# Squared-ReLU attention into a gated feed-forward block on one core: the third batch's transposing DMAs in a chain, its later loads one by one over the second batch, and two score buffers through the third batch

## The chip, the core and the metric

The kernel runs on one core of a Trainium2 chip. The metric is the time of one execution on the device in microseconds (us), median of several runs. Of the kernel before there are five runs, and one more execution that was profiled.

## The reference, cut to what matters

```python
# q, k, v: (8 batches, 12 heads, 448 rows, 64) float32
scores = (1 / sqrt(64)) * q @ k.T
attn = maximum(scores, 0) ** 2 / 448
x = (attn @ v), heads side by side: (8 * 448, 768)
# w_gate, w_val: (768, 1536); w_out: (1536, 768)
out = (gelu(x @ w_gate) * (x @ w_val)) @ w_out      # (3584, 768) float32
```

There is no softmax: a score needs nothing but its own square after the ReLU. The kernel works in bf16 with sums in float32.

## The kernel before, in words

**Stages and tiles.** The code counts batches b from 0 to 7, so the third batch is b = 2; heads are taken in pairs (pr 0 to 5), and two pairs make a group m (0 to 2). A batch passes through these steps:

- GpSimd issues the loads that cast to bf16: `load_qk` (L205; one DMA for q or for k and four heads, all in tile `qk16`) and `load_v` (L220; two DMAs for four heads of v).
- q and k are transposed. In batches 0 and 1 (`b < EARLY`, and `EARLY` is 2) TensorE does it (`add_transposes`, L362). From batch 2 on `add_dma_transposes` (L251) does it: VectorE copies a group from `qk16` into `qkr` (L261; one buffer for all batches), and then SyncE issues two transposing DMAs from `qkr` into `qkT` (L265), one of four and one of three chunks of 64 rows. The units of the group's scores wait for both.
- `add_scores` makes 21 units of scores for a batch (`NU`; units 0 to 6 belong to group 0, 7 to 13 to group 1, 14 to 20 to group 2). Each goes into a score buffer of two PSUM banks; ScalarE applies the ReLU (L425), VectorE squares (L431).
- `add_values` (L459) multiplies by v, a pair at a time; VectorE writes the result into `xT` (L487).
- `add_gate_value` (L519) makes gate and value for each of 12 slices `fc` of the hidden width. ScalarE applies the GELU (L538) and VectorE multiplies (L543); that multiply is `u_op[b, fc]`.
- `add_out` (L572) makes output tiles t of 128 rows in two halves g. ScalarE copies each half from PSUM (L598, `cp`), and after the second half SyncE issues two stores (L603). `osb` has four buffers.

**Two rows of work on TensorE.** Matmuls use 64 x 64 tiles of the array. The lower and upper halves of the rows get separate streams, `PE0` and `PE1`, which follow one another through a PSUM bank: the first half of a sum is made by the lower rows, the second by the upper rows (`then`, L351). While the upper rows finish one bank, the lower rows begin another.

**What sets the order.** All is planned in Python before anything is emitted. Every step of work has a place `at` in planned time (L657 to L705), in which only the feed-forward matmuls count: `starts[b]` is where batch b's feed-forward work begins, and the units of a batch's scores are spread evenly between `lo` and `hi` of L677 to L685. So attention for batch b + 1 lies among the feed-forward work for batch b. `run_plan` (L23) then plays the plan through with a cost for each operation and assumed arrival times of the DMAs. The streams `PE0` and `POOL` (GpSimd's loads) keep their listed order; from the lists of `PE1`, ScalarE, VectorE and SyncE it takes whichever operation is ready first. The order in which it takes them is the order of each engine's program, and every engine keeps to it. A DMA's assumed lateness is the `lag` of an operation, and the operation `wait` on the pretended engine `IDLE` (L254) puts a further 2 or 5 us ahead of a `qkr` copy in the plan. It exists in the plan alone.

**PSUM.** Eight banks: score buffer 0 (two banks), four banks F for all other results in a ring, and score buffer 1 (two banks). When the list `wide` is filled (L446), the kernel goes over to one score buffer, and the two banks of the other join as X, so that results go round six banks (`next_bank`, L302; `next_scores`, L316). Before the change that happens at the last unit of batch 1.

**Loads around the change.** The q and k of batch 2's groups 0 and 1 are issued at the end of the start-up loads (L652). Those of group 2 are issued after the copies of output tile 0, and v of batch 2 after tile 1 and after the multiplies of `fc` 1 and 3 of batch 1 (L613 to L616, L562). Each waits for that copy or multiply. Loads for batch 3 are issued after the even `fc` of batch 1 (q and k in turn, L557), and its v after `fc` 7, 9 and 11 (L564). The transposes of batch 2 are entered just ahead of its first scores (L709).

Of the kernel before, what the change touches and what calls it, by code (L numbers as in the profile page):

```python
# [88 lines left out]
def kernel(  # L89
# [16 lines left out]
    B, H, S, D = q.shape  # L106
# [4 lines left out]
    NM = NPAIR // 2  # L111
    NU = SC * NPAIR // 2
# [12 lines left out]
    EARLY = 2  # L125
# [33 lines left out]
    SYNC = mybir.DependencyInfo(mybir.DependencyClass.Sync, mybir.DependencyReason.DATA)  # L159
# [17 lines left out]
    w12_op, wo_op, head_op = {}, {}, {}  # L177
# [61 lines left out]
    qkT, tr_op = {}, {}  # L239
# [7 lines left out]
        return t.rearrange("d (m c r) x -> d m c r x", m=NM, c=SC)  # L247

    qkr = {}

    def add_dma_transposes(b, m):  # L251


        wait = Op("IDLE", 2.0 if b == EARLY else 5.0, lambda: None,  # L254
                  [head_op[b, pr, i] for pr in (2 * m, 2 * m + 1) for i in range(2)])
        IDLE.append(wait)

        def emit_copy():
            if b not in qkr:
                qkr[b] = lpool.tile([128, NM, SC, 4, D], bf16, name="qkr", tag="qkr")  # L260
            nc.vector.tensor_copy(  # L261
                qkr[b][:, m], qk16[b].rearrange("p (h c d) -> p c h d", c=SC, d=D)[:, :, 4 * m:4 * m + 4])

        def emit_transpose(c0, c1):
            ins = nc.sync.dma_start_transpose(  # L265
                by_group(qkT_tile(b))[:, m, c0:c1].rearrange("d c r x -> d (c r) x"),
                qkr[b][:, m, c0:c1].rearrange("p c h d -> p (c h d)"))
            if b > EARLY:

                if c0:  # L270
                    tc.add_manual_dep(ins.ins, one[0].ins.name, SYNC, reason="pace")
                one[:] = [ins]

        one = []
        copy = Op("DVE", 0.65, emit_copy, [wait, *tr_op.get((b - 1, m), ())], lag=0.15, prio=3)
        DVE.append(copy)
        tr_op[b, m] = [Op("SP", 0.19 * 2 * (c1 - c0), lambda c0=c0, c1=c1: emit_transpose(c0, c1),
                          [copy, last_s.get(b - 2)], lag=4.5) for c0, c1 in ((0, VC), (VC, SC))]
        if b > EARLY:
            tr_op[b, m][1].deps.append(tr_op[b, m][0])  # L280
        SP.extend(tr_op[b, m])


# [114 lines left out]
    def add_scores(at, b, u):  # L398


        m, w = divmod(u, SC)
        tail = w == VC - 1
        prs = (2 * m, 2 * m + 1) if tail else (2 * m + (w > VC - 1),)
        cl = w if w < VC else w - VC
        box = {}
        n, free = next_scores()

        def emit(j, pr):
            if not box:
                box[0] = psS[n].tile([128, 2, 512], f32, name="sp", tag="S")  # L410
            sp = box[0]
            t = by_group(qkT_tile(b))[HALF[j], m, :, pr % 2, :]
            for i in range(2):
                if tail:
                    n0 = (pr % 2) * S // 2
                    qs = t[:, :, i * P // 2:(i + 1) * P // 2]
                    mm(sp[HALF[i], j, n0:n0 + S // 2].rearrange("k (c p) -> k c p", c=SC),
                       t[:, VC - 1, HALF[1]], qs, j, i, True, True)
                else:
                    mm(sp[HALF[i], j, 0:S].rearrange("k (c p) -> k c p", c=SC),  # L420
                       t[:, cl + i * VC, HALF[1]], t[:, :, HALF[0]], j, i, True, True)

        def emit_relu():
            rl = box[1] = rpool.tile([128, 2, S], bf16, name="rl", tag="rl")
            nc.scalar.activation(rl[:, :, :], box[0][:, :, 0:S], AF.Relu)  # L425

        def emit_sq():
            a = apool.tile([128, 2, S], bf16, name="attnT", tag="attnT")
            for pr in prs:
                att[b, pr, VC - 1 if tail else cl] = a  # L430
            nc.vector.tensor_tensor(a[:, :, :], box[1][:, :, :], box[1][:, :, :], op=ALU.mult)  # L431

        if b < EARLY:
            have = [t_op[b, m, pr % 2] for pr in prs]
        else:
            have = tr_op[b, m]
        have = [*have, *free]
        ops = [[Op(f"PE{j}", 0.095 if tail else 0.189, lambda j=j, pr=pr: emit(j, pr), have, lag=0.24)
                for pr in prs] for j in range(2)]
        last_s[b] = ops[1][-1]  # L440
        relu = Op("ACT", 0.8, emit_relu, [ops[0][-1], ops[1][-1], *sq_list[-4:-3]], lag=0.18, prio=2)
        n_a = len(sq_list)
        sq = Op("DVE", 0.54, emit_sq, [relu, *att_free[n_a - 12:n_a - 11]] if n_a >= 12 else [relu],
                lag=0.2, prio=2)
        scores_read(n, relu)
        if (b, u) == (EARLY - 1, NU - 1):  # L446
            wide.append(0)
        sq_list.append(sq)
        att_free.append(None)
        for pr in prs:  # L450
            sq_op.setdefault((b, pr), []).append((sq, n_a))
            sq_of[b, pr, VC - 1 if tail else cl] = sq
        ACT.append(relu)
        DVE.append(sq)
        both(at, zip(*ops))
# [60 lines left out]
    GS, RS = 0.189, 0.1625  # L516
    PLACE5 = -7.0

    def add_gate_value(at, b, fc, g):  # L519

        i, o = divmod(fc * 128, WCH)
        w = (wg, wv)[g][i]
        box = {}
        half, free = next_bank()

        def emit(r, dc):
            if not box:
                box[0] = new_bank(done, half=half)
            if r == 1 and dc == 0:
                wait_lower(box)  # L530
            for j in range(2):
                ins = mm(box[0][HALF[j], 0:S], w[HALF[r], dc, o + P * j:o + P * (j + 1)],
                         xT[b][HALF[r], dc, :], r, j, r == 0 and dc == 0, r == 1 and dc == KC - 1)
            box[1] = ins

        def emit_gelu():
            gel[b, fc] = gpool.tile([128, S], bf16, name="gel", tag="gel")
            nc.scalar.activation(gel[b, fc][:, :], box[0][:, 0:S], AF.Gelu)  # L538

        def emit_mult():  # L540
            if fc == 0:
                uT[b] = upool.tile([128, FC, S], bf16, name="uT", tag="uT")
            u_op[b, fc].ins = nc.vector.tensor_tensor(  # L543
                uT[b][:, fc, :], gel.pop((b, fc))[:, :], box[0][:, 0:S], op=ALU.mult).ins

        ops = [[Op(f"PE{r}", GS, lambda r=r, dc=dc: emit(r, dc),
                   [w12_op[i][g], x_op[b, dc], *(free if r == 0 and dc == 0 else ())], lag=0.24)
                for dc in range(KC)] for r in range(2)]
        if g == 0:
            done = gel_op[b, fc] = Op("ACT", 0.55, emit_gelu, [ops[1][-1]], lag=0.06, prio=0)  # L550
            ACT.append(done)
        else:
            done = u_op[b, fc] = Op("DVE", 0.54, emit_mult, [gel_op[b, fc], ops[1][-1]],
                                    lag=0.2, prio=0)
            DVE.append(done)
            if b + 2 < B and b:
                if fc % 2 == 0:  # L557
                    m, i = divmod(fc // 2, 2)
                    load_qk(b + 2, i, 4 * m, 4 * m + 4, [done])
                    if i:  # L560
                        add_dma_transposes(b + 2, m)
                elif b == 1 and fc < 5:  # L562
                    load_v(2, 2 * fc + 2, 2 * fc + 6, [done])
                elif fc > 6:  # L564
                    h0 = 2 * (fc - 7)
                    load_v(b + 2, h0, h0 + 4, [done])
        bank_read(half, done)
        if (b, fc) == (0, 0):
            at = [PLACE5 - 0.5 + 0.1 * g] * 3 + [0.01 * g] * 3
        then(at, GS, *ops, done)  # L570

    def add_out(at, t, g):  # L572
# [37 lines left out]
        cp = Op("DVE" if last else "ACT", 0.48, emit_copy, [ops[1][-1]], prio=1)  # L610
        bank_read(half, cp)
        (DVE if last else ACT).append(cp)
        if t == 0:  # L613
            load_qk(2, g, H - 4, H, [cp])
        elif (t, g) == (1, 0):
            load_v(2, 0, 4, [cp])  # L616
        if last and g != 1:

            part = slice(bounds[g and g - 1], bounds[g + 1])
# [40 lines left out]
    starts = []  # L660
# [14 lines left out]
    LEAD = 6.0  # L675
    LO1 = 2.0
    for b in range(B):  # L677
        if b == 0:
            lo, hi = -60.0, -12.0
        elif b == 1:  # L680
            lo, hi = LO1, starts[1] - LEAD
        elif b == 2:
            lo, hi = starts[1] + 6.0, starts[2] - LEAD
        else:
            lo, hi = starts[b - 1] - LEAD, starts[b] - LEAD  # L685
        step = (hi - lo) / NU
# [19 lines left out]


    for at, _, fn, args in work:
        if fn is add_scores and args == (2, 0):  # L709
            for m in range(NM):  # L710
                add_dma_transposes(2, m)
        fn(at, *args)


# [15 lines left out]
    for kind, lo, hi in pairs:  # L730
        if kind == "with":
            upper.append((tau[place[lo]], hi))
        else:
# [5 lines left out]
            t = tau[behind + 1]  # L739
# [48 lines left out]
```

## Time and profile before

| | us |
|---|---|
| median of five runs | 427.3 (425.7 to 428.2) |
| the profiled execution, its own time | 425.15 |
| its span, first to last instruction | 423.4 |

| in the profiled execution | start, us |
|---|---|
| multiplies of batch 1, fc = 0, 1, 2, 4, 7, 11 (L543) | 79.2, 81.7, 84.4, 89.5, 98.1, 109.6 |
| ReLU of batch 2's score units 0, 7, 14, 20 (L425) | 81.9, 94.4, 107.3, 118.1 |
| ReLU of batch 3's units 0, 7, 14 | 120.8, 136.7, 152.4 |
| copies into qkr for batch 2 (L261) | 67.9, 72.6, 78.2 |
| copies into qkr for batch 3 | 93.5, 104.9, 116.3 |
| transposing DMAs of batch 2 (L265) | 69.1, 73.4, 75.5, 77.4, 81.2, 83.5 |

The granted clock of TensorE is 0.998 of full speed over the span. In what follows a line of a wait gives the total wait in us, how often, and the longest; a line of a timeline or a chain gives start and length in us. A group's length runs from the start of its first instruction to the end of its last, so neighbouring groups overlap, since a matmul of 349 ns shares the array with others. A line of stretches gives the stretch, its length, and then for each engine busy us and, in brackets, the instructions.

### The profile page before, as it was taken

Reading aid. Unit: us, or ns where it says so; the run is one execution under the profiler, and the core shown is the slowest. Engines: PE = TensorE matmul, PEld = TensorE weight load, DVE = VectorE, ACT = ScalarE, POOL = GpSimd, SP = SyncE. Lnnn points to the kernel's source line nnn. Section 1 sums busy time; section 2 is a strip of 40 time slices with the busy share of each in tenths; the row PEclk is TensorE's granted clock in tenths of the full one; section 3 lists DMA queues with packets and bytes.
Section 4 is the critical chain, followed back from the end, with each engine's and each line's share of the span. In section 5 each row is a group of like instructions: output and inputs, shape, how many; then the busy total and the mean of one; then the engine's idle time right before and its main releaser. Section 6 shows DMA issues by size and latency. Waiting matters only on the chain.

```text
span 423.4 us, 19612 instructions
## 1 busy us (share of the span) xinstructions
PE 415.7 (98%) x9087; PEld 378.6 (89%) x9090; DVE 213.9 (51%) x347; ACT 223.7 (53%) x320; POOL 73.6 (17%) x120
## 2 busy tenths in 40 slices
PE   8999999999999999999999999999999999999996
PEld 3558778799999999999999989999999989999995
DVE  3876665266544665446643666446743555212201
ACT  4956663466556655556555665556555556322220
POOL 8645401223100131012300122011310000000000
PEclk9999999999999999999999999999999999999999
DMA  7999998999974399645974389645994100120034
GB/s 100 191 200 197 199 209 140 197 142 113 118 127 93 47 115 118 135 68 71 140 130 107 52 91 134 140 73 70 121 147 97 39 4 3 47 71 3 2 77 115
DMA packets 75281, 44.91 MB, mean 106 GB/s; under 512 B 36160, under 2 KB 71744, under 8 KB 75200
## 3 DMA queue, kind: packets, MB, share of 16 engines
q0 software_dynamic: 37152, 24.39, 43.2%
q1 hardware_dynamic: 37888, 19.08, 25.4%
q8 instruction: 71, 1.16, 1.2%
q10 hardware_dynamic: 160, 0.20, 0.1%
q14 instruction: 10, 0.08, 0.1%
HBM read 48.76 MB, written 11.01 MB: 141 GB/s over the span
## 4 chain that ended last, share of the span: by engine, by line
PE 93%; DMA 3%; POOL 1%; ACT 1%; issue 0%; DVE 0%; SPq 0%; POOLq 0%
PE ff L162 84%; PE sp L162 8%; DMA qkT<-qkr 2%; DMA qk<-in_k_dram 2%; PE sp L377 1%; POOL qk L214 1%; PE ff L377 1%; ACT rl L425 0%; PE ff L340 0%; SPq L603 0%; DVE qkT L381 0%; DVE attnT L431 0%; ACT osb L598 0%; DVE osb L598 0%; POOL ident masks.py:199 0%
## 5 line engine op out<-in xcount | busy, mean ns | idle before, releaser
L425 ACT ACTIVATE rl<-sp 128x896 bf16<-128x896 f32 x168 | 152.4, 918 | 93.0 <-PE sp L162 84.3
L162 PE MATMUL ff<-xT,wg 64*64 64x448 bf16 x2304 | 199.0, 349 | 0.0
L162 PE MATMUL ff<-xT,wv 64*64 64x448 bf16 x2304 | 197.9, 349 | 0.0
L162 PE MATMUL ff<-wo,uT 64*64 64x384 bf16 (+1 forms) x2736 | 151.5, 320 | 0.0
L431 DVE TENSOR_TENSOR attnT<-rl 128x896 bf16<-128x896 bf16 x168 | 104.0, 623 | 70.0 <-ACT rl L425 67.1
L162 PEld LDWEIGHTS <-wv 64*64 64x64 bf16 x2304 | 126.7, 107 | 6.9
L162 PEld LDWEIGHTS <-wg 64*64 64x64 bf16 x2304 | 125.5, 107 | 7.6
L162 PEld LDWEIGHTS <-uT 64*64 64x64 bf16 x2736 | 128.8, 107 | 3.1
L162 PE MATMUL sp<-qkT 64*64 64x448 bf16 (+1 forms) x768 | 105.3, 328 | 1.8 <-DMA qkT<-qkr 1.0
L543 DVE TENSOR_TENSOR uT<-gel,ff 128x448 bf16<-128x448 bf16 x96 | 59.5, 620 | 70.1 <-PE ff L162 63.2
L162 PE MATMUL ff<-attnT,v 64*64 64x448 bf16 (+1 forms) x768 | 88.5, 326 | 0.1
L538 ACT ACTIVATE gel<-ff 128x448 bf16<-128x448 f32 x96 | 52.0, 542 | 46.1 <-PE ff L162 45.6
L162 PEld LDWEIGHTS <-qkT 64*64 64x64 bf16 x768 | 46.2, 106 | 11.1 <-issue 5.6
L598 ACT COPY osb<-ff 128x384 f32<-128x384 f32 x54 | 25.7, 477 | 52.5 <-PE ff L162 52.5
L162 PEld LDWEIGHTS <-v 64*64 64x64 bf16 x768 | 47.8, 107 | 3.5 <-issue 1.1
L487 DVE TENSOR_SCALAR xT<-ff 128x448 bf16<-128x448 f32 x48 | 29.9, 623 | 34.0 <-PE ff L162 34.0
L214 POOL DMA_DIRECT2D qk<-in_q_dram x25 | 15.5, 621 | 125.9 <-DVE uT L543 105.6
L227 POOL DMA_DIRECT2D v<-in_v_dram x48 | 29.5, 621 | 42.7 <-DVE uT L543 33.2
L214 POOL DMA_DIRECT2D qk<-in_k_dram x25 | 15.4, 615 | 61.2 <-DVE uT L543 52.7
L261 DVE COPY qkr<-qk 128x1792 bf16<-128x1792 bf16 x18 | 19.4, 1078 | 4.5 <-DMA qk<-in_k_dram 4.5
L598 DVE COPY osb<-ff 128x192 f32<-128x192 f32 (+1 forms) x3 | 1.2, 422 | 17.9 <-PE ff L162 17.9
L377 PEld LDWEIGHTS <-qk 128*64 128x64 bf16 x168 | 5.2, 110 | 3.2 <-issue 3.1
(23 smaller groups left out, 41.7 us busy)
## 6 DMA issues: line engine op xcount, KB each, us to landing
out_dram<-osb SPq DMA_DIRECT2D x54, 192.0 KB, 2.8
v<-in_v_dram POOLq DMA_DIRECT2D x48, 128.0 KB, 4.9
qk<-in_q_dram POOLq DMA_DIRECT2D x23, 224.0 KB, 4.6
qk<-in_k_dram POOLq DMA_DIRECT2D x23, 224.0 KB, 5.3
wg<-in_moe_w_gate_dram POOLq DMA_DIRECT2D x6, 384.0 KB, 10.5
wv<-in_moe_w_val_dram POOLq DMA_DIRECT2D x6, 384.0 KB, 11.4
wo<-in_moe_w_out_dram POOLq DMA_DIRECT2D x4, 576.0 KB, 15.2
qkT<-qkr SPq DMA_TRANSPOSE x36, 4.7
```

The source lines that it names most:

```text
L162: return nc.tensor.matmul(o, lhsT, rhs, start=start, stop=stop, tile_position=(P * row, P * col))
L214: op = load(4 * (h1 - h0) * S * D, lambda: nc.gpsimd.dma_start(tile_of().rearrange("p (h x) -> p h x", h=H)[:, h0:h1, :], src[b, h0:h1].re ...
L227: return nc.gpsimd.dma_start(v16[b][HALF[i], h0:h1, :, :], v[b, h0:h1].rearrange("h (p c) d -> p h c d", c=SC)[:, :, c0:c0 + VC, :])
L261: nc.vector.tensor_copy(qkr[b][:, m], qk16[b].rearrange("p (h c d) -> p c h d", c=SC, d=D)[:, :, 4 * m:4 * m + 4])
L377: nc.tensor.transpose(t[HALF[j], c, :], src[:, 2 * (2 * m + r) + j, c, :], ident[:, :], tile_position=(0, P * j))
L425: nc.scalar.activation(rl[:, :, :], box[0][:, :, 0:S], AF.Relu)
L431: nc.vector.tensor_tensor(a[:, :, :], box[1][:, :, :], box[1][:, :, :], op=ALU.mult)
L487: nc.vector.tensor_scalar_mul(xT[b][:, pr, :], box[0][:, 0:S], scalar1=out_scale)
L538: nc.scalar.activation(gel[b, fc][:, :], box[0][:, 0:S], AF.Gelu)
L543: u_op[b, fc].ins = nc.vector.tensor_tensor(uT[b][:, fc, :], gel.pop((b, fc))[:, :], box[0][:, 0:S], op=ALU.mult).ins
L598: cp.ins = (nc.vector.tensor_copy if last else nc.scalar.copy)(osb[t][:, cols], box[0][:, 0:N]).ins
```

## The change

It has four parts.

1. *Transposes.* The list `one`, which holds the last transposing DMA, outlives a call. In batch 2 the DMAs of groups 1 and 2 each wait until the transposing DMA before them has landed, across groups too; group 0's two do not wait for one another. Later batches keep what they had: the second DMA of a group waits for the first. A call can be given operations (`deps`) that its planned wait comes after.
2. *Loads.* A table `LATE` names, for 17 places in the plan (copies of output tiles 0 to 5 and multiplies of batch 1), one load each, or one call of `add_dma_transposes`, or both. The last number of an entry says which: 0 for q, 1 for k, 2 for v, 3 for the transposes alone. So batch 2's third group of q and k comes after `fc` 0 and 1 of batch 1, its v after `fc` 2, 5 and 8, and batch 3's loads after `fc` 6, 7 and 9 and then after output tiles 2 to 5. Batch 2's transposes are entered at the copies of tiles 0 and 1 and at `fc` 4.
3. *Score buffers.* `wide` is filled at the last unit of batch 2 in place of batch 1: two score buffers and four F banks through batch 2.
4. *Place.* The units of batch 2's scores lie between `starts[1] + 8.0` and `starts[2] - 6.0`, where they began at `starts[1] + 6.0`.

```diff
-    def add_dma_transposes(b, m):
+    one = []
+    def add_dma_transposes(b, m, deps=()):
         wait = Op("IDLE", 2.0 if b == EARLY else 5.0, lambda: None,
-                  [head_op[b, pr, i] for pr in (2 * m, 2 * m + 1) for i in range(2)])
+                  [*deps] + [head_op[b, pr, i] for pr in (2 * m, 2 * m + 1) for i in range(2)])
...
-            if b > EARLY:
-
-                if c0:
-                    tc.add_manual_dep(ins.ins, one[0].ins.name, SYNC, reason="pace")
-                one[:] = [ins]
-
-        one = []
+            if b > EARLY and c0 or m and b == EARLY:
+                tc.add_manual_dep(ins.ins, one[0].ins.name, SYNC, reason="pace")
+            one[:] = [ins]
...
-        if b > EARLY:
+        if m or b > EARLY:
             tr_op[b, m][1].deps.append(tr_op[b, m][0])
+        if m and b == EARLY:
+            tr_op[b, m][0].deps.append(tr_op[b, m - 1][1])
...
-        if (b, u) == (EARLY - 1, NU - 1):
+        if (b, u) == (EARLY, NU - 1):
             wide.append(0)
...
+    LATE = {(0, 0): (2, 0, 3), (1, 0): (2, 1, 3), 0: (2, 2, 0), 1: (2, 2, 1), 2: (2, 0, 2),
+            4: (2, 2, 3), 5: (2, 1, 2), 6: (3, 0, 0), 7: (3, 0, 1), 8: (2, 2, 2), 9: (3, 1, 0),
+            (2, 0): (3, 1, 1), (3, 0): (3, 0, 2), (3, 1): (3, 2, 0), (4, 0): (3, 2, 1),
+            (5, 0): (3, 1, 2), (5, 1): (3, 2, 2)}
+
+    def load_late(b, m, i, done):
+        if i < 2:
+            load_qk(b, i, 4 * m, 4 * m + 4, done)
+        elif i == 2:
+            load_v(b, 4 * m, 4 * m + 4, done)
+        if i == 3 or i == 1 and b > EARLY:
+            add_dma_transposes(b, m, done if m else ())
...
-            if b + 2 < B and b:
+            if b == 1:
+                if fc in LATE:
+                    load_late(*LATE[fc], [done])
+            elif b + 2 < B and b:
                 if fc % 2 == 0:
                     m, i = divmod(fc // 2, 2)
                     load_qk(b + 2, i, 4 * m, 4 * m + 4, [done])
                     if i:
                         add_dma_transposes(b + 2, m)
-                elif b == 1 and fc < 5:
-                    load_v(2, 2 * fc + 2, 2 * fc + 6, [done])
...
-        if t == 0:
-            load_qk(2, g, H - 4, H, [cp])
-        elif (t, g) == (1, 0):
-            load_v(2, 0, 4, [cp])
+        if (t, g) in LATE:
+            load_late(*LATE[t, g], [cp])
...
-            lo, hi = starts[1] + 6.0, starts[2] - LEAD
+            lo, hi = starts[1] + 8.0, starts[2] - LEAD
...
-        if fn is add_scores and args == (2, 0):
-            for m in range(NM):
-                add_dma_transposes(2, m)
```

## The prediction

> **What bounds the kernel now.** I read the page first, then TensorE's waits, the chain that ended last, the timelines of TensorE and SyncE around the longest wait, and last the stretches of the span beside one another. The page's first part, then the one wait of TensorE that comes after the start-up, then the chain around it (start, length, what):
>
> ```profile
> PE 415.7 (98%) x9087; PEld 378.6 (89%) x9090; DVE 213.9 (51%) x347; ACT 223.7 (53%) x320; POOL 73.6 (17%) x120
> ```
> ```profile
> PE sp L162 <- DMA qkT<-qkr: 1.0, 1, 1.0
> ```
> ```profile
> 71.39 0.49 ACT osb L598
> 71.88 0.02 issue
> 71.89 0.54 SPq L603
> 72.44 0.05 issue
> 72.48 0.92 SPq L603
> 73.40 0.04 issue
> 73.45 7.55 DMA qkT<-qkr
> 81.00 0.04 issue
> 81.05 0.38 PE sp L162 x2
> ```
>
> TensorE is the bound, and it is left alone by the other engines except in one place: the scores of batch 2 (b = 2, the third) wait for its first pair of transposing DMAs (m = 0). The chain says why they are late: the second of the pair was issued only at 73.45, behind two stores of an output tile on SyncE, and took 7.55 us to land. TensorE's timeline there:
>
> ```profile
> 77.96 1.35 PE L162 MATMUL ff<-xT,wg 64*64 64x448 bf16 x24
> 79.10 0.97 PE L162 MATMUL ff<-xT,wv 64*64 64x448 bf16 x12
> 81.05 0.38 PE L162 MATMUL sp<-qkT 64*64 64x448 bf16 x2 [0.97 <-DMA qkT<-qkr]
> ```
>
> The reader is to see more than the 0.97 us. From 77.96 to 79.10, 24 matmuls start in 1.14 us: 47.4 ns for one of 448 columns when both row halves of the array are fed. From 79.10 only 12 start until 81.05: the planner had already left the lower rows without work. 12 x 47.4 ns is 0.57 us of work in 1.95 us, so the place costs **1.38 us**, not 0.97.
>
> The second place is not an idle gap. Two equal stretches of 50 us (busy time and matmuls of TensorE first):
>
> ```profile
> 82.00:132.00 50.00, 50.00 (x1126) 47.48 (x1122) 28.56 (x46) 32.07 (x45) 9.15 (x15) 1.00 0.90 126
> 182.00:232.00 50.00, 50.00 (x1139) 48.37 (x1134) 26.63 (x42) 28.11 (x41) 7.06 (x12) 1.00 0.66 101
> ```
>
> Taken by tile, both hold 384 output matmuls and 98 and 99 value matmuls; the first holds 120 of scores against 98, and so 524 of gate and value against 558. 34 x 47.4 ns less and 22 of scores more (some 8 of them of half width, 0.85 us together) make 0.76 us less work done in the first stretch. There batch 2's attention runs on one score buffer, with a relu each 1.7 us; in the later stretch they come each 2.1 to 2.5 us apart. From 52 to 64, with two score buffers and four other banks, 268 matmuls fall in 12 us: some 252 x 47.4 + 16 of half width x 23.7 ns is 12.3 us, nothing lost.
>
> **What the Trainium skill says.** The Trainium skill's page "Perfetto Trace Analysis", section "Identifying the Most-Contended Engine", warns that matmul busy time says little of the distance to the limit. The trace agrees: PE reads 50.00 busy in both stretches above, and only the counts differ. The same page, "Optimization Strategy", says that a bubble that keeps coming back can mean too few buffers; the 1.7 us beat of the scores is such a candidate, though no row of the trace names it. The Trainium skill's page "DMA: Bandwidth & Descriptors", section "Issuing engines are not separate DMA queues", says that DMAs of all issuers share the same 16 engines and interleave. The trace agrees: the transposes between 60 and 92, which overlap one another and the loads, need 6.8 us in the median from issue to landing, and all 36 of the run 4.7 (3.0 to 7.6).
>
> **The change part by part.** *The chain in batch 2.* Six DMAs stay six. m = 0's two have no added wait; m = 1's first now waits until m = 0's second has landed, and each later one for the one before. So at 73.45 the late one is alone: with the run's median it lands at 78.2 instead of 81.0. Queued behind each wait on SyncE are the next transposes and the stores of tiles 0 and 1 (L603); a store has four osb buffers, so a few us there cost nothing. m = 1: 78.2 + 4.7 + 4.7 = 87.6; its scores, unit 7, had their relu at 94.4. m = 2: its copy now follows the multiply of fc = 4 (89.5 before, some 1.8 earlier now) by 2 us, so 90; plus 1.1 for the copy and 9.4 for two DMAs is 100.5; unit 14 had its relu at 107.3. Both are in time by 5 us or more.
>
> *The start of batch 2's scores, 2 planned us later* (`starts[1] + 8.0` for 6.0). Planned time counts feed-forward matmuls at full rate, so 2 us more of them come first. TensorE then wants the first scores at 80.05 + 2.0 = 82.05, 3.9 us after 78.2. The place's cost goes: **-1.38 us**. The order moves work and adds none.
>
> *Two score buffers through batch 2* (and four F banks in place of six until its end). The stretch from 52 to 64 is that arrangement at a like density (21 units over 27 planned us there, over 28.8 here) and loses nothing. Of the 0.76 us I take two thirds, **-0.5 us**; the ends are -0.8 and +0.8. The bad end: about 38 bank fills lie in this stretch, and a wait of 0.04 us in each, at half the array (38 x 0.04 / 2), would eat 0.76 us. Of four banks under attention and output tiles together the trace shows nothing.
>
> *The loads moved.* Each is one 0.61 us issue on GpSimd, which is busy 17% and waits in order. The third group of q and k of batch 2 goes from behind the output copies of tile 0 (issued 70.2 and 72.2) to fc = 0 and 1, about 80 and 82. This frees VectorE, which stood 4.51 us at 78.18 waiting for that k; the page names nobody who waited for that, so I cost it at nothing. v of batch 2's first four heads goes from 74.8 to fc = 2: issued by 84.5, landed by 90.3 (5.8 in that window), wanted at 91.8. Cover 1.5 us or a little more. Batch 3's first k goes from 85.3 to fc = 7 (98.1 before, about 97.2 now). In the trace its copy follows a k issue by 8.2 to 9.0 us (93.5, 104.9 and 116.3 after 85.3, 96.3 and 107.3), so 106; the copy takes 1.1; the second transpose followed the first by 3.5 to 5.4 us and lands 4.7 later: 115.3 to 117.2. The first scores of batch 3 are wanted at about 120.4 (0.4 ahead of the relu at 120.8) - 1.9 = 118.5. In time by 1.3 to 3.2 us. m = 1 starts from the copy of output tile 2 (112.8, now 111): copy 120, landed 131, wanted near 134. m = 2 from tile 4 (123.4, now 121.6): landed by 141, wanted near 150, and the single qkr buffer is free before batch 4's copy (147.4, now 145.5). For friction here I add **+0.3 us** (0 to 3.5): the planner's own waits are longer than the measured ones, and where it believes in lateness it leaves half the rows unfed.
>
> Sum against the profiled execution: 425.15 - 1.38 - 0.5 + 0.3 = 423.6 us (its span is 423.4, with 1.75 us around it). The median of the runs is 427.3, 2.15 above it; the same difference of -1.6 gives **425.7 us**.
>
> **The rivals.** *The stall moves instead of going (0.2).* SyncE's order is the planner's. If it puts tile 1's stores (ready at 77.3) ahead of m = 0's second transpose as well, this is issued near 78.9 and lands at 83.6, 1.5 us after it is wanted; or v of batch 2 comes that late. Then only the buffers' 0.5 is left, less the friction: 427.1 us. Against it: the two are released by the same copy, and tile 0's stores alone stood between. That the buffers do nothing, or the change doesn't do what it says, ends here too.
>
> *Batch 3's first transposes come late: slower (0.14).* TensorE takes its work in order, so lateness is paid in full. The two DMAs now share the engines with batch 2's v loads and the stores; at 7.6 us each, the run's longest, 107.1 + 15.2 = 122.3, 3.8 us after 118.5. Less the 1.9 gained until then makes +1.9: 429.2 us. It turns slower from a landing after 120.4, and slower by 0.3% from 121.7. For it: 13 us of lead are given away. Against it: in later batches the second of a pair is issued 3.1 to 5.4 us after the first (148.5 and 151.6, 159.2 and 162.8), so such a pair is down in 8 to 10 us.
>
> **How the numbers follow.** The forecast has 0.66: between -0.9 and -2.4 us, from the ends of the terms. This kernel's measurement can tell about 0.3%, 1.28 us, from no change; three quarters of the forecast's chance, 0.5, lie beyond. So faster 0.52 (a little for a rival that turns out well), same 0.34 (the rest of the forecast and the first rival), slower 0.14. Range 424.6 to 428.0: the low end is all 1.38 + 0.76 of gain and half a us of the runs' scatter (425.7 to 428.2); the high end takes in the first rival and the milder part of the second.
>
> **What would show it.** Right: TensorE's wait on qkT gone; transposes of batch 2 near 4.7 us apart, each landing before its scores; 24 matmuls per 1.14 us right up to the first scores near 82; relus of batch 2 closer than 1.7 us; no wait before the first scores of batch 3. Wrong: a new wait of TensorE on qkT near 118, or on v near 92; fewer matmuls from 82 to 118 although no gap shows, which would be the four banks.

## The result, and the profile after

The kernel after takes 425.89 us (median of 36 runs, 423.91 to 428.49), the kernel before, run beside it, 426.11 us (71 runs, 424.29 to 429.17). The ratio is 0.9988, with a 95% interval of 0.9977 to 0.9999: about half a us gained by the ratio, 0.2 by the medians, where 1.6 were forecast. The interval hardly leaves out 1, and the gain is under the 0.3% that the forecast asked for a change: by that bound the time is the same, which had a chance of 0.34 against 0.52 for faster. 425.89 lies in the range. That it also lies close to 425.7 is luck: over 71 runs the kernel before is 1.2 us below the median of the five that the forecast started from, and this makes up for most of the gain that is missing.

The medians hide that the times of the kernel after fall into two groups: 12 of the 36 lie from 423.9 to 424.94, 24 from 425.47 up. The profiled execution belongs to the upper one: 426.25 us, span 424.5. Some executions of most kernels here, one of these 36 and up to six of 22 below (the profiled one of experiment 6 among them), have a granted clock of 0.990 to 0.995 in place of 0.996 to 1.000 and take over 427.5 us, and no difference below rests on them.

First TensorE in the page, then all its waits of 0.5 us or more (total, times, longest):

```profile
PE 415.7 (98%) x9087; PEld 369.8 (87%) x9090; DVE 213.8 (50%) x347; ACT 224.1 (53%) x320; POOL 73.8 (17%) x120
```
```profile
PE ff L162 <- issue: 1.6, 1, 1.6
PE ff L762 <- DVE table L151: 1.2, 1, 1.2
PE ff L377 <- DMA qk<-in_k_dram: 0.9, 2, 0.7
PE sp L162 <- ACT rl L425: 0.5, 2, 0.3
```

The wait on qkT is gone. In its place stands one for "issue": nothing that the profile's semaphores show. The chain where the wait used to be has only TensorE in it, up to the first scores of batch 2 at 82.6:

```profile
65.57 17.20 PE ff L162 x362
82.77 0.18 PE sp L162 x2
```

and TensorE's timeline around 80, the place of the old hole, is filled:

```profile
79.95 1.29 PE L162 MATMUL ff<-xT,wv 64*64 64x448 bf16 x20
...
81.09 1.29 PE L162 MATMUL ff<-xT,wg 64*64 64x448 bf16 x20
...
82.57 0.38 PE L162 MATMUL sp<-qkT 64*64 64x448 bf16 x2
```

The new hole is at 141. The same timeline there:

```profile
138.87 0.67 PE L162 MATMUL ff<-xT,wv 64*64 64x448 bf16 x7
141.15 0.56 PE L162 MATMUL ff<-xT,wv 64*64 64x448 bf16 x5 [1.62 <-issue]
```

Seven matmuls of value sums run, then nothing starts for 1.97 us, then the sums go on with the same operands. The kernel emits these matmuls in pairs, with no wait inside a pair, and the last one before the hole, at 139.19, is the first of a pair: the break is in the middle of it. So it is not data that was lacking, and what is left is instructions. The view of the DMA queues between 131.0 and 138.4, queue by queue (packets, MB, share of the engines), in the kernel before:

```profile
q0 software_dynamic: 272, 0.23, 26.8%
q1 hardware_dynamic: 160, 0.39, 20.6%
q8 instruction: 1, 0.02, 1.0%
```

and after:

```profile
q1 hardware_dynamic: 1844, 0.82, 67.2%
q0 software_dynamic: 1066, 0.61, 59.8%
```

Queue q8 brings instructions, 71 packets of 16 KB in the whole run. The page counts 9,087 matmuls and 9,090 weight loads on TensorE, together 18,177, and 71 x 256 is 18,176, so a packet is 256 of them, some 5.8 us of work (the 71 begin between 15 and 420 us). In the kernel after none arrives from 131.0 to 138.4 (they begin at 130.6 and 138.5), while transposes, stores and loads move more than twice the bytes of before. A count that follows experiment 12 shows that the holes lie at the ends of such blocks. The Trainium skill's page "Runtime: NRT & Kernel Launch", section "Instruction fetch mechanics", says that the instruction memory is refilled in blocks of 16 KiB, 256 instructions, by the sequencer's own DMA queue, and that the cost is mostly hidden. The trace agrees on the block, and here the cost is not hidden.

To see where all time went I took each matmul at 46.7 ns for 448 columns and in proportion (no 10 us of the traces beat that by more than 0.03 us) and counted what a stretch lacks. Us lost:

| stretch | before | after |
|---|---|---|
| 64 to 78 | 0.72 | 1.19 |
| 78 to 82 (the wait on qkT) | 1.43 | 0.08 |
| 82 to 107 | 0.60 | 0.38 |
| 107 to 118 (dense scores) | 0.80 | 0.33 |
| 118 to 132 | 0.16 | 0.32 |
| 132 to 142 | 0.20 | 2.30 |
| sum | 3.91 | 4.60 |

Up to 132 the change gives back 3.71 - 2.30 = 1.4 us, and from 132 to 142 it loses 2.1. The start of this execution was 0.4 us slower by 32 us, which is not put down to the change: in experiment 1 the same kernel lost 0.7 us less there than here.

### The profile page after: what moved, and what is told of

It reads as the page before. It is cut to its first block, busy times and chain, and to the rows that moved or that the text cites. A ratio compares the mean times of both kernels' runs of the same rounds, so it can differ in the third digit from the quotient of the medians.

```text
span 424.5 us, 19605 instructions
## 1 busy us (share of the span) xinstructions
PE 415.7 (98%) x9087; PEld 369.8 (87%) x9090; DVE 213.8 (50%) x347; ACT 224.1 (53%) x320; POOL 73.8 (17%) x120
## 4 chain that ended last, share of the span: by engine, by line
PE 95%; DMA 2%; POOL 1%; issue 1%; ACT 0%; DVE 0%; POOLq 0%
PE ff L162 86%; PE sp L162 8%; DMA qk<-in_k_dram 2%; PE sp L377 1%; POOL qk L214 1%; PE ff L377 1%; ACT rl L425 0%; PE ff L340 0%; DVE qkT L381 0%; DVE attnT L431 0%; DVE osb L613 0%; POOL ident masks.py:199 0%; POOL ident masks.py:197 0%; POOLq L782 0%
## 5 line engine op out<-in xcount | busy, mean ns | idle before, releaser
L162 PE MATMUL ff<-xT,wv 64*64 64x448 bf16 x2304 | 195.6, 349 | 1.6 <-issue 1.6
L162 PE MATMUL ff<-xT,wg 64*64 64x448 bf16 x2304 | 196.8, 349 | 0.0
L162 PEld LDWEIGHTS <-wv 64*64 64x64 bf16 x2304 | 123.4, 107 | 12.2 <-issue 2.6
L162 PEld LDWEIGHTS <-wg 64*64 64x64 bf16 x2304 | 122.3, 107 | 11.1 <-issue 0.5
L162 PE MATMUL sp<-qkT 64*64 64x448 bf16 (+1 forms) x768 | 107.5, 328 | 0.8 <-ACT rl L425 0.5
```

The source lines that it names most:

```text
L162: return nc.tensor.matmul(o, lhsT, rhs, start=start, stop=stop, tile_position=(P * row, P * col))
```

## The experiments

Times are medians; a ratio is to the kernel before in the same series, with its 95% interval. "Lost" is counted as above. A threshold of 425.0 us, chosen after the times of the kernel after were seen, is used to say how many executions fall in the upper group.

**1. The kernel after again**, unaltered.

> The changed kernel once more, nothing altered. Its profile has one hole of TensorE, 1.97 us between two matmuls of gate and value near 141 us, with no semaphore behind it; a 16 KB transfer of the instruction queue began at 138.5, just before the hole ends, 7.9 us after the one before it, where some 5.7 us is usual. Theory (late instructions, because batch 3's loads of v, its transposes and the stores now crowd the DMA engines from 127 to 138): the hole comes back at the same place in a new execution, within 2 us of 141, and most executions lie near 426.2 with a smaller group near 424.1. Rival (chance: such a hole may fall anywhere in any kernel): this profile shows no hole there, or one at another place, and the times are spread without two groups.

423.84 us, ratio 0.9953 (0.9930 to 0.9977), 3 of 10 above 425.0. The profiled execution (423.66) has no hole: 0.20 us lost from 132 to 142, 2.39 from 64 to 132. So the hole is not in each execution, and without it the kernel is 1.5 to 2 us faster. The expectation of a hole at the same place failed for this profile, and it could not tell the two theories apart.

**2. Batch 3's v loads earlier.**

```diff
+            10: (3, 0, 2), 11: (3, 1, 2), (2, 1): (3, 2, 2),
-            (2, 0): (3, 1, 1), (3, 0): (3, 0, 2), (3, 1): (3, 2, 0), (4, 0): (3, 2, 1),
-            (5, 0): (3, 1, 2), (5, 1): (3, 2, 2)}
+            (2, 0): (3, 1, 1), (3, 1): (3, 2, 0), (4, 0): (3, 2, 1)}
```

> The changed kernel with batch 3's three v loads moved from output tiles 3 and 5 (issued 117 to 131 us) to fc 10, fc 11 and tile 2 (about 106 to 116), all else as it is. Theory (late instructions by crowding): no hole near 139 to 141, the instruction transfers stay under 7 us apart there, and the median falls by about 1.5 to 2 us against the changed kernel, to 424.1 to 424.7; ratio to the kernel before 0.995 to 0.997. Rival (chance): the hole stays or the median remains at about 425.9, ratio 0.999.

424.25 us, ratio 0.9963 (0.9950 to 0.9976), 4 of 22 above 425.0, no hole in the profile. The median is the expected one, but on that chip the kernel after itself had gone as fast, so this alone shows nothing of the cause.

**3. The second score buffer alone**, on the kernel before.

```diff
-        if (b, u) == (EARLY - 1, NU - 1):
+        if (b, u) == (EARLY, NU - 1):
```

> The kernel before with the second score buffer kept to the end of batch 2, nothing else. My forecast's step: about 0.5 us gained between 86 and 118 us, the wait of 1.38 us near 80 still there; ratio 0.998 to 0.9995. Rival (four banks for the other results cost as much as the second buffer gives): no gain from 86 to 118, ratio 1.000 or above.

425.9 us, ratio 0.9995 (0.9978 to 1.0012), 12 of 14 above 425.0: no gain. From 107 to 118 it loses 0.57 in place of 0.80. No wait on qkT is listed, since other matmuls still run, but the late transpose lands at 81.07, the first scores start at 81.11, and 0.83 us are lost from 78 to 82. To this come 1.11 at a hole of "issue" at 95.9 that the first profile of the kernel before doesn't have.

**4. The later place alone**, on the kernel before.

```diff
-            lo, hi = starts[1] + 6.0, starts[2] - LEAD
+            lo, hi = starts[1] + 8.0, starts[2] - LEAD
```

> The kernel before with batch 2's scores 2 planned us later (starts[1] + 8.0), nothing else: transposes unchained, one score buffer, loads as before. If the second transposing DMA still lands at 81 us, the scores wanted at 82 no longer wait, so the later place alone would give back the 1.38 us: ratio 0.9965 to 0.998, and the chain of the DMAs would not be what removes the wait. If the planner then moves that DMA later too, or the denser units on one score buffer cost it again, ratio 0.999 to 1.001.

425.74 us, ratio 1.0003 (0.9985 to 1.0020), 16 of 22 above 425.0. The late transpose lands at 81.0 as before, but the first scores now start at 82.0: the wait on qkT is gone completely (nothing lost from 78 to 82). The time is the same: 0.54 us are lost from 82 to 86, where the units are denser, and 1.53 from 94 to 98 at a hole of "issue". A wait that vanishes without a gain, with a hole 15 us later, made me ask what the kernel before does in most of its executions.

**5. The kernel before again**, unaltered.

> The kernel before once more, nothing altered. Its times lie in two groups, near 424.9 and near 426.3. Theory (late instructions, crowding): the upper group is executions in which TensorE runs out of instructions where batch 3's loads and batch 2's transposes are densest in this kernel, near 93 to 97 us, as in the two kernels made from it; the profile shows a hole of 1 to 1.6 us there if it falls in the upper group (time above 425.5) and none if in the lower. Rival: a time above 425.5 without a hole, so the two groups have another cause.

426.02 us, ratio 1.0011 (0.9988 to 1.0034), 17 of 22 above 425.0. The profiled execution, 426.07, is from the upper group and shows what the first profile didn't. Its waits of TensorE in the span (nothing on qkT), and its timeline:

```profile
PE ff L752 <- DVE table L151: 1.2, 1, 1.2
PE ff L162 <- issue: 0.9, 1, 0.9
PE ff L162 <- ACT rl L425: 0.2, 1, 0.2
PE sp L162 <- ACT rl L425: 0.2, 1, 0.2
```
```profile
94.43 0.35 PE L162 MATMUL ff<-xT,wv 64*64 64x448 bf16 x1
95.69 0.72 PE L162 MATMUL ff<-xT,wv 64*64 64x448 bf16 x9 [0.91 <-issue]
```

Its DMA queues from 85.0 to 92.8 hold no instruction packet either, and the loads beside them take long to land (the last number of the lower lines, us):

```profile
q0 software_dynamic: 867, 0.53, 77.3%
q1 hardware_dynamic: 1866, 0.47, 73.4%
...
qk<-in_k_dram POOLq DMA_DIRECT2D x1, 224.0 KB, 10.6
...
qkT<-qkr SPq DMA_TRANSPOSE x1, 9.5
```

So the kernel before has the same trouble at another place: where its own loads, transposes and stores are dense, 84 to 93. In this execution the late transpose lands at 80.71 and the first scores start at 80.75; 0.36 us are lost from 78 to 82 and 1.25 from 94 to 98, in the first profile 1.43 and 0.13. So in these two profiles it pays about the same in sum, in two forms. It would be easy to say that a TensorE that stands still at 80 lets its instructions get ahead and so is spared the hole at 95. The traces don't bear this out: when the packet near 84.5 begins, TensorE has got equally far into its blocks in both (269 and 272 matmuls and weight loads started beyond 256 for each earlier packet). They part with the next packet, which begins at 90.7 in the first profile and at 93.0 here. Why is not shown.

**6. The stretch from 128 to 139 made busier**: two of batch 3's v groups are loaded twice in the kernel after, the second time into tiles that nobody reads.

```diff
             load_v(b, 4 * m, 4 * m + 4, done)
+            if b > EARLY and m:
+                load_again(b, 4 * m, 4 * m + 4, done)
```

> The changed kernel with the last two groups of batch 3's v loads (issued about 127 to 131 us) made twice, the second copy into tiles that nobody reads; four DMAs of 128 KB more, so the work is the reference's and a little beside it. Theory (late instructions by crowding): the stretch from 128 to 139 is busier, the hole near 139 to 143 comes in nearly all executions or is longer, median 426 to 427.5, ratio to before 1.000 to 1.003. Rival (chance): as often as without them, so a median of 423.8 to 424.5 with a smaller upper group, ratio 0.995 to 0.997.

428.54 us, ratio 1.0035 (1.0010 to 1.0061), 21 of 22 above 425.0. TensorE's waits:

```profile
PE sp L162 <- DMA qkT<-qkr: 2.3, 1, 2.3
...
PE ff L162 <- issue: 0.4, 1, 0.4
```

512 KB of traffic in that place put nearly all executions into the upper group, and the median is above the 426 to 427.5 that were expected. Against the eighth kernel, which has the same late loads without it (and no chain in batch 2) and ran in the same series (425.26), the median is 3.3 us higher. The cause is not only late instructions: the larger wait is for batch 3's second group of transposes, at 136.6, with a hole of 0.75 us at 143.5 after it. The rival, chance, which expected no more than without the traffic, falls.

**7. Batch 3's loads all earlier**, on the kernel after.

```diff
-            (2, 0): (3, 1, 1), (3, 0): (3, 0, 2), (3, 1): (3, 2, 0), (4, 0): (3, 2, 1),
-            (5, 0): (3, 1, 2), (5, 1): (3, 2, 2)}
+            10: (3, 1, 1), 11: (3, 2, 0), (2, 1): (3, 2, 1), (3, 0): (3, 0, 2), (3, 1): (3, 1, 2),
+            (4, 0): (3, 2, 2)}
```

> The changed kernel with all loads of batch 3 earlier: k of its second group at fc 10, q and k of its third at fc 11 and output tile 2, v at tiles 3 and 4, so that the loads end near 125 and the transposes near 131, before batch 4's loads begin at 132. Theory (late instructions by crowding): no hole from 130 to 143, hardly any upper group, median 423.7 to 424.3, ratio 0.994 to 0.997. It would fail if the traffic, now denser from 104 to 124, makes a hole there: then a new hole near 115 to 125 and a median near 426.

424.10 us, ratio 0.9961 (0.9945 to 0.9976), 4 of 22 above 425.0. From 132 to 142 only 0.24 us are lost; 0.51 are from 126 to 132, at a short hole at 126.6, just after the stretch that the traffic has moved to.

**8. Without the chain**, the rest of the kernel after kept.

```diff
-            if b > EARLY and c0 or m and b == EARLY:
+            if b > EARLY and c0:
...
-        if m or b > EARLY:
+        if b > EARLY:
             tr_op[b, m][1].deps.append(tr_op[b, m][0])
-        if m and b == EARLY:
-            tr_op[b, m][0].deps.append(tr_op[b, m - 1][1])
```

> The changed kernel without the chain: batch 2's six transposing DMAs wait for nothing but their copies and buffers, as before the change; loads, place and buffers stay changed. My forecast gave the chain the landing at 78.2 in place of 81.0 and so part of the 1.38 us. If group 1's copy alone (now after output tile 1) already keeps the DMAs apart, or the later place covers a landing at 81, nothing is lost: no wait of TensorE on qkT, work lost from 64 to 132 within 0.3 us of the changed kernel's 2.3 to 2.4. If the chain is what gives it, TensorE waits on qkT again near 80 to 82, about 1 us more lost.

425.26 us, ratio 0.9982 (0.9962 to 1.0002), 14 of 22 above 425.0; the profiled execution is a lower one, 423.88. No wait on qkT, 2.26 us lost from 64 to 132. The chain is not what removes the wait: group 0's second transpose, issued at 73.48, lands in 3.6 us, since group 1's copy comes after output tile 1 anyway and its transposes don't start before 78.75. This kernel has the late loads and many upper executions (14 of 22), the seventh in the same series hasn't (4 of 22).

**9. One score buffer again** in the kernel after.

```diff
-        if (b, u) == (EARLY, NU - 1):
+        if (b, u) == (EARLY - 1, NU - 1):
```

> The changed kernel with one score buffer in batch 2 again (and six banks for the rest), the other parts kept. My forecast gives the second buffer 0.5 us of the gain. If that is so, 0.3 to 0.7 us more are lost from 64 to 132 than the changed kernel's 2.3 to 2.4, most of it from 107 to 118. If units that are now denser throttle TensorE on one buffer, it is more than 1 us. If the four banks cost what the buffer gives, nothing.

424.61 us, ratio 0.9984 (0.9968 to 1.0000), 8 of 22 above 425.0. 3.18 us are lost from 64 to 132: 0.59 from 82 to 86 (0.03 with two buffers) and 0.67 from 107 to 118 (0.33). From 82 to 118, where the two kernels differ in their banks, 1.8 us are lost in place of 0.7, so with the denser units the second buffer saves about 1 us in these profiles. On the kernel before, where the units are not so dense, experiment 3 had 0.80 - 0.57 = 0.2 us from 107 to 118. The median is no higher than that of the kernel after in the same series (425.06, experiment 11), because fewer executions are above 425.0; those below it have a median of 424.4 here and of 423.9 there.

**10. The earlier place again** in the kernel after.

```diff
-            lo, hi = starts[1] + 8.0, starts[2] - LEAD
+            lo, hi = starts[1] + 6.0, starts[2] - LEAD
```

> The changed kernel with batch 2's scores back at starts[1] + 6.0. The chain lets the second transposing DMA of group 0 land near 78; the scores are wanted near 80 then. If the chain or the later copy of group 1 gives the early landing, there is no wait of TensorE on qkT and the place is worth nothing (work lost from 64 to 132 within 0.3 us of 2.3 to 2.4). If the DMA lands after 80, up to 1.4 us are lost there again and the place is what removes the wait.

424.75 us, ratio 0.9974 (0.9958 to 0.9989), 10 of 22 above 425.0. Group 0's second transpose lands at 78.4 and the first scores start at 80.0; next to nothing is lost from 78 to 82, 2.54 from 64 to 132. So the place isn't needed either once group 1's transposes come later: either of the two removes the wait. The profiled execution, an upper one (426.32), waits 1.4 us for batch 3's qkT at 136.7, after a hole of 0.70 us that ends at 133.4.

**11. The kernel after a third time.**

> The changed kernel a third time, beside the next one on the same chip. Theory (late instructions by crowding from 127 to 138): two groups of times, near 424 and near 426, with a good share in the upper; median between 423.9 and 426.0 according to that share; a profile above 425.5 has a hole or holes between 130 and 145, one below has none. Rival (chance): holes at other places.

425.06 us, ratio 0.9963 (0.9945 to 0.9982), 11 of 22 above 425.0. The profiled execution is an upper one, 426.27. It shows both costs. The chain from 120.9 on (start, length, what), and the line of the wait:

```profile
120.92 0.66 ACT rl L425
121.58 8.05 DMA qkT<-qkr
129.63 0.02 issue
129.65 5.91 DMA qkT<-qkr
135.55 0.14 issue
135.69 0.38 PE sp L162 x2
...
140.48 0.71 issue
```
```profile
PE ff L162 <- issue: 0.9, 2, 0.7
PE sp L162 <- DMA qkT<-qkr: 0.8, 1, 0.8
```

The first transposing DMA of batch 3's group 1 takes 8.05 us and the second 5.91, so the scores that want them at 134.9 wait until 135.7, and the hole of "issue" comes at 141.2. Lost from 132 to 142: 2.77 us.

**12. The earlier loads of experiment 7 again**, beside 11 on the same chip.

> The changed kernel with batch 3's loads earlier, as in the seventh run, beside the changed kernel on the same chip. Theory (late instructions by crowding): fewer executions above 425.0 than for the changed kernel, at most a quarter, median 423.8 to 424.3, ratio 0.994 to 0.997. Rival (chance): the same share as the changed kernel.

424.39 us, ratio 0.9946 (0.9925 to 0.9967), none of 10 above 425.0. From 132 to 142, 0.15 us lost. In matmuls that fall in that stretch (in brackets after PE), first the kernel of 11, then this one:

```profile
132.00:144.00 12.00, 10.35 (x210) 7.78 (x205) 6.37 (x11) 5.48 (x8) 1.22 (x2) 1.00 1.00 149
```
```profile
132.00:144.00 12.00, 12.00 (x269) 11.50 (x263) 7.04 (x12) 6.92 (x10) 1.22 (x2) 1.00 0.58 102
```

The numbers at the end are the DMA engines' share and GB/s: 1.00 and 149 against 0.58 and 102. Over all runs the kernel after lies above 425.0 in 38 of 68, the one with earlier loads in 4 of 32.

**The count that ties the holes to the packets.** If TensorE stops because the next packet hasn't come, it must stop at the same place of a block of 256 each time. A view of stretches from 0 into a hole gives the matmuls and weight loads started before it. They are 5,555 in the recorded profile, 3,512 in experiments 3 and 4, 3,511 in 5, 5,558 in 6 and 11, and 5,303 in 10 (the hole of 0.70 us). Divided by 256 these leave 179 to 184, in all seven. Where TensorE waits for transposes the remainder is another: 114 in the first profile of the kernel before, 248 in experiments 6, 10 and 11. And each of the seven holes ends 1.4 to 1.8 us after the transfer of a packet has ended. This leaves chance no room.

The same count separates the two costs in the upper profiles, by the time without a start. The recorded one has the lack of instructions alone (1.97 us). Experiment 10 has 0.70 us of it and 1.75 of waiting for transposes, experiment 11 has 1.06 and 1.13 (and a short hole of 0.51 at the end of a block at 132.5), and experiment 6, with the added traffic, 0.75 and 2.60.

## Why the prediction came out as it did

- *The wait at 80 (-1.38).* The mechanism and the size are right for the execution that I read: 1.43 us lost there before, 0.08 after, and the late DMA, now issued at 73.75, landed in 4.8 us, at 78.6 where 78.2 was expected. But the reason was not the chain, as experiment 8 shows. The chain's four DMAs took 7.0, 6.0, 5.5 and 4.5 us where 4.7 was forecast, and were in time all the same. And the wait is not the same in each execution of the kernel before: 0.36 us in experiment 5, whose profile loses 1.25 at the hole near 95 instead. That hole is in none of the ten profiles with batch 3's loads moved (at most 0.12 us lost from 94 to 98). So the credit was right and its account was that of one execution.
- *Two score buffers (-0.5).* Right in direction: 0.47 us from 107 to 118 and 0.22 from 82 to 107, together with the denser place; alone on the kernel before it gave 0.2 from 107 to 118 and no gain in time (experiment 3), and taken out of the kernel after it costs about 1 us in the profile (experiment 9). So the sign is shown, the 0.5 is not. The four banks cost nothing that shows. The forecast's own yardstick was a little off: the stretch from 52 to 64, said to lose nothing, lacks 0.2 us at the 46.7 ns used here.
- *v of batch 2 in time.* Right: no wait there in any profile. Batch 3's first transposes landed by 115.7, as forecast (115.3 to 117.2).
- *The loads moved, "friction" +0.3.* This is the step that failed, and it is a term that was sized too small, though its stated ends, 0 and 3.5, hold it. It measured about 2 us in the upper part of the executions and nearly nothing in the others: 2.30 us lost from 132 to 142 in the recorded profile, 2.77 in experiment 11, 0.20 in experiment 1. I had taken 4.7 us for a transposing DMA to land and 3.5 to 5.4 for the second to follow, figures from where the loads were in the kernel before. Moved beside loads and stores, the first of group 1 took 7.6 us in the recorded profile and 8.05 in experiment 11: "landed 131, wanted near 134" became 134.4 (129.6 and 4.8 us) and 135.6. In experiment 1, which lost nothing here, the pair landed at 133.9, 0.2 us before the scores that need it. And I had asked of each transfer only who waits for its data. The instruction packets are in the same account of the 16 engines, and nobody is named as waiting for them. The reason that I gave for the friction, the planner's own waits, is not what the profiles show.
- *The rival of late transposes* had a part of the mechanism and the right batch, at group 1 in place of group 0: it is there in experiments 10 and 11, while in the recorded profile instructions alone are late. The two together take back the gain in about half of the executions without making the kernel slower. I had priced the lateness of group 0 alone.
- In numbers: 1.4 us gained up to 132, where the forecast's two credits make 1.9, less some 2 us in a third to two thirds of the executions. Three series of the kernel after gave 0.9988, 0.9953 and 0.9963, according to that share. Where the load of the engines is taken off 128 to 139, the whole forecast gain is there: 0.9946 and 0.9961.

What stays open: why the share of upper executions differs from series to series (24 of 36, 3 of 10, 11 of 22), what decides in one execution whether a packet comes late, and what the kernel before does in its fastest executions (424.2 to 425.0), of which there is no profile.

## What to carry to other kernels

When loads are moved out of one crowded stretch, look at what the stretch that receives them holds, transposing DMAs and instruction packets included, and price a transfer by its landing under that load, not by its median over the run. A wait in one profile of a kernel whose times spread over 1% may be only one of the forms in which it pays; take a second profile before crediting its removal. And where TensorE stops in the middle of a sum for "issue", look at the DMA queue that brings instructions, and count the instructions up to the stop: the same remainder by 256 at each stop tells this cause from others.

## What was not expected of the hardware

- TensorE can run out of instructions in straight code: seven holes of 0.70 to 1.97 us (the recorded profile and experiments 3, 4, 5, 6, 10 and 11), each at the same place of a block of 256 and ending 1.4 to 1.8 us after a 16 KB packet has come. The packets that ended them began 6.9 to 10.6 us after the ones before, where 5.8 us lie between two in the mean. The time between packets alone is no sign: 8.9 us in experiment 7 cost only the 0.5 us at 126.6, since TensorE was further from the end of its block when that gap began (175 matmuls and weight loads started beyond 256 for each earlier packet, against 338 at 130.6 in the recorded profile).
- A transposing DMA that lands in 2.8 us at best (recorded profile) took 8.05 us beside loads and stores in experiment 11, and 12.3 with the added loads of experiment 6.
